# Reordering the first five blocks of a fused dynamic convolution and squared-ReLU FFN: one load, one exp and the softmax and product steps between the units

## The chip, the cores and the metric

One core of one Trainium2 chip runs the whole program. The metric is the device time of one execution in microseconds (us). A run has a median over three to eleven executions. Ratios compare the runs of two kernels in the same rounds, so they are not quite the ratio of the medians that are quoted beside them. Each has a 95% interval. "The changed kernel" is the kernel after the change, "before" the kernel before it.

## The reference

```python
w = exp(weight_gen - max); w = w / (sum(w) + 1e-9)           # (8, 4096, 8 heads, 7 taps)
out[b,s,h,g] = sum_k w[b,s,h,k] * x_pad[b, s+k, h, g]        # causal window of 7, D = 192
h = maximum(out.reshape(32768, 192) @ w_in, 0.0)             # (192, 2048)
y = (h * h) @ w_out                                          # (2048, 192), float32 out
```

## The kernel before

The 32,768 tokens are cut into 64 sub-blocks of 512. Blocks 0 and 1 hold one sub-block, every later one two. One block goes through these steps:

- softmax of a part of `weight_gen` on ScalarE (exp, "E") and VectorE (sum, reciprocal, scale, "S"). The result `v` is moved as rows into `wr` by DMA;
- VectorE multiplies `wr` with a mask into bands `bd` ("B" and the sub-block's number);
- TensorE multiplies bands with x into `yp` ("C"), ScalarE copies it to `y`;
- 16 units "u" (8 in blocks 0 and 1): TensorE makes `h`, ScalarE the ReLU `t`, VectorE the square `g`;
- "M": TensorE multiplies half of the hidden tiles `g` of 256 tokens with `w_out` into `o`, as a rule for an earlier block; after every second M ScalarE copies one PSUM bank out and VectorE adds the other (blocks 0 and 1 use one bank and need no sum).

The digit after E, S, L (load) is the softmax part. Plans fix the order by hand for the first blocks, and all engines work through their share of that order without skipping ahead. A ring is a pool of buffers used in turn: who wants the next buffer waits until its last reader is done. The gate is a one-column copy on GpSimd that waits for a load and so holds back the loads that GpSimd issues after it. What the argument touches:

```python
p_t1 = ctx.enter_context(tc.tile_pool(name="p_t1", bufs=5))      # the t ring
ps_h = ...(name="ps_h", bufs=3, space=PSUM)                      # h and yp share three slots
ps_o = ...(name="ps_o", bufs=1, space=PSUM)                      # one pair of o banks
# ... start of the program, after the weights of part 0 and w_in ...
        x_load_f32(1)                                   # second x, sync queue
        nc.scalar.copy(out=w_i[:, 1, 0], in_=w_st[1])
        cross_w_in(1)
        s1.load(nc.sync)                                # weights of softmax part 1
        for i in (0, 2, 1, 3, 4):
            st_band(0, (i,))
        st_conv(0)                                      # C of block 0, then the first y copy
        nc.gpsimd.tensor_copy(out=gate, in_=x_st[1][:, 0:1])   # GpSimd waits for the second x
        for q in range(4):
            load_w_out(q, 4)                            # 1.5 MB, GpSimd queue, behind the gate
        s2.load(nc.gpsimd)
        x_load(2)
# ... a softmax part that is done: its rows go to wr on the sync and the GpSimd queue in turn
        move_rows(s)
# a unit
        nc.scalar.activation(out=t1, in_=h, func=ActF.Relu)
        nc.vector.tensor_tensor(out=g, in0=t1, in1=t1, op=AluOp.mult)
```

The softmax here doesn't subtract the row's maximum and nothing guards it: scores larger than these inputs give would overflow.

Of the kernel before, what the change touches and what calls it, by code (L numbers as in the profile page):

```python
# [9 lines left out]
def kernel(  # L10
# [26 lines left out]
    nc = tc.nc  # L37
# [96 lines left out]
    def cross_w_in(q):  # L134
        for r0, r1 in ((0, RT), (RT, 0)):
            nc.sync.dma_start(out=w_i[r0 : r0 + RT, q, 1], in_=w_i[r1 : r1 + RT, q, 0])

    def cross_w_in_by_pe(q):
        n = NQ + NQ // 2
        for a in range(0, n, 2 * TB):  # L140
            b = min(a + 2 * TB, n)
            pt = ps_h.tile([P, 2 * TB], f32, name="pt", tag="h")
            for c in range(a, b, TB):
                nc.tensor.matmul(
                    out=pt[:, c - a : c - a + TB], lhsT=swap, rhs=w_i[:, q, 0, c : c + TB],
                    start=True, stop=True,
                )
            nc.scalar.copy(out=w_i[:, q, 1, a:b], in_=pt[:, 0 : b - a])
# [137 lines left out]
    def block_load(j, dst, src, width, eng):  # L286
        t0 = (j % NBB) * TB
        first, last = int(t0 == 0), NT
        if first:
            eng.dma_start(out=dst[:, 0], in_=src[0:P, :])  # L290
        a = t0 + tile_start(j, NT - 1)
        if a != t0 + starts[-1]:
            last = NT - 1
            eng.dma_start(out=dst[:, last], in_=src[a : a + P, :])
        ap = rows(src, t0 + starts[first], width)
        ap = bass.AP(
            tensor=ap.tensor, offset=ap.offset,
            ap=[ap.ap[0], [STEP * width, last - first], ap.ap[2]],
        )
        eng.dma_start(out=dst[:, first:last], in_=ap)  # L300
# [5 lines left out]
    def x_load_f32(j):  # L306
        x_st[j] = p_one.tile([P, (R + HALO) * HK], f32, name="x_st", tag="ex")
        block_load(
            j, x_st[j][:, 0 : NT * D].rearrange("p (t d) -> p t d", t=NT), x[j // NBB], D, nc.sync
        )  # L310
# [199 lines left out]
    with nc.allow_low_precision("fp16 matmul pipeline"), tc.manual_schedule():  # L510
# [26 lines left out]
        def spin(n):  # L537
            for i in range(n):
                nc.tensor.matmul(out=wp, lhsT=warm[:, 0:P], rhs=warm, start=True, stop=True)  # L539

        s0, s1, s2 = parts[:3]
# [19 lines left out]
        x_cast(0, nc.scalar.copy)  # L561
        cross_w_in_by_pe(0)
        spin(14)
        x_load_f32(1)
        nc.scalar.copy(out=w_i[:, 1, 0], in_=w_st[1])
        cross_w_in(1)
        s1.load(nc.sync)
        for i in (0, 2, 1, 3, 4):
            st_band(0, (i,))
        st_conv(0)  # L570
# [2 lines left out]
        for q in range(4):  # L573
# [6 lines left out]

        steady = "MuMuuu" * 3 + "MuuuMCu"
        plans = {
            0: "B1 X1 u u u E1 S1 u C u u u u",
            1: "L3 u u B2 M E2 B3 u M E2 u u S2 u M u C u S2 M",
            2: "L4 u u u E3 M u u u M B4 u u u u M B5 S3 u u u u M u E3 C u",
            3: "L5 L6 M S3 u u u M u u u u M u M B6 E4 u u u M M B7 u u S4 u E4 M u C M u",
        }


# [45 lines left out]
        for j in range(len(plans), NBLK):  # L635
            plan, u = [], 0
# [55 lines left out]
        for j in range(NBLK):  # L692
            if j + 2 < NBLK:
                load_rows(j + 2)
            u = 0
# [71 lines left out]
```

## Time and profile before

| | before |
|---|---|
| time, median of 3 (lowest to highest) | 748.35 us (748.23 to 749.56) |
| span of the profiled execution | 746.6 us |
| first unit of block 0 begins at | 15.55 us |
| blocks 0, 1, 2, 3, 4, 5 take | 8.03, 13.25, 18.12, 22.63, 23.40, 22.52 us |
| a steady block | 22.55 us |

A block's time is the distance from its first matmul of the plan to the next block's. TensorE is the bound, so what a block takes over the pace of its matmuls shows as a TensorE wait, whose releaser names who caused it, or as a slot that is longer than usual (the view of waits leaves out gaps under 0.15 us).

### The profile page before, as it was taken

What the parts mean: (1) busy time and instruction counts of PE and PEld (TensorE: products, weight loads), DVE (VectorE), ACT (ScalarE), POOL (GpSimd) and SP (SyncE); (2) the same over time, 40 slices, a digit from 0 to 9 for tenths busy, and PEclk for the clock granted to TensorE, in tenths of its full rate; (3) what the DMA queues carried; (4) which work ended last, traced back from release to release, by engine and by line L of the source; (5) the groups of instructions that cost most, each with busy time, mean ns of one, the idle gap of its engine ahead of it and who ended that gap; (6) DMA issues with size and microseconds to landing.
All of it is one profiled execution on the core that took longest, in us unless ns stands there. A gap on an engine that the chain in (4) does not pass through costs nothing.

```text
span 746.6 us, 33289 instructions
## 1 busy us (share of the span) xinstructions
PE 739.0 (99%) x15106; PEld 556.5 (75%) x15106; DVE 621.8 (83%) x1001; ACT 624.7 (84%) x755; POOL 88.8 (12%) x130
## 2 busy tenths in 40 slices
PE   8999999999999999999999999999999999999998
PEld 4767877877777777777777777787777777777787
DVE  5999998998889888888889888898888987677853
ACT  5998788888888888888888888888888888888874
POOL 7321220101101100011000110001100011001000
PEclk9999999999999999999999999999999999999999
DMA  8654454436554234644245542365441354441312
GB/s 223 112 106 109 80 101 85 100 70 139 94 118 79 75 57 80 140 79 73 45 74 139 102 65 53 51 139 108 59 80 48 57 108 80 60 73 51 51 46 65
DMA packets 122169, 64.81 MB, mean 87 GB/s; under 512 B 83849, under 2 KB 118636, under 8 KB 121516
## 3 DMA queue, kind: packets, MB, share of 16 engines
q1 hardware_dynamic: 77708, 45.66, 22.4%
q0 software_dynamic: 44176, 16.93, 20.5%
q8 instruction: 118, 1.93, 1.1%
q14 instruction: 23, 0.19, 0.1%
q10 hardware_dynamic: 144, 0.10, 0.0%
HBM read 48.61 MB, written 28.70 MB: 104 GB/s over the span
## 4 chain that ended last, share of the span: by engine, by line
PE 94%; DVE 2%; issue 1%; DMA 1%; ACT 1%; POOL 0%; DVEq 0%; ACTq 0%
PE o L475 45%; PE h L441 43%; PE yp L416 6%; DVE g L453 1%; DVE bd L348 1%; DMA wr<-v_first 0%; DMA wg<-in_weight_gen_dram 0%; POOL wr L330 0%; ACT t L450 0%; DVE v_first L239 0%; ACT ex L217 0%; DVE ssum L224 0%; DVE rcp L231 0%; DVE o_sb L491 0%; ACT y L427 0%
## 5 line engine op out<-in xcount | busy, mean ns | idle before, releaser
L450 ACT ACTIVATE t<-h 128x1024 f16<-128x1024 f32 x512 | 496.7, 1026 | 65.6 <-PE h L441 65.3
L453 DVE TENSOR_TENSOR g<-t 128x1024 f16<-128x1024 f16 x512 | 334.3, 687 | 100.5 <-ACT t L450 97.8
L475 PEld LDWEIGHTS <-g 64*128 64x128 f16 (+1 forms) x8032 | 352.3, 94 | 55.0 <-issue 4.8
L475 PE MATMUL o<-w_o,g 64*128 64x192 f16 (+1 forms) x8032 | 385.3, 243 | 0.9 <-DVE o_sb L491 0.6
L441 PE MATMUL h<-y,w_i 64*128 64x512 f16 (+1 forms) x3168 | 379.7, 370 | 2.2 <-ACT t L450 0.9
L441 PEld LDWEIGHTS <-w_i 64*128 64x128 f16 x3168 | 162.6, 94 | 117.2 <-issue 5.2
L348 DVE TENSOR_TENSOR bd<-wr,mask 128x4160 f16<-128x4160 f16 (+3 forms) x89 | 149.3, 1701 | 4.0 <-DMA wr<-v_first 4.0
L300 POOL DMA_DIRECT2D xt<-in_x_dram x62 | 51.2, 830 | 446.7 <-PE yp L416 423.7
L489 ACT COPY o_sb<-o 128x384 f32<-128x384 f32 x129 | 62.2, 482 | 33.8 <-PE o L475 33.8
L491 DVE TENSOR_TENSOR o_sb<-o,o_sb 128x384 f32<-128x384 f32 x123 | 68.2, 555 | 8.4 <-ACT o_sb L489 5.6
L427 ACT CAST y<-yp 128x1024 f16<-128x1024 f32 (+1 forms) x64 | 48.1, 803 | 14.5 <-PE yp L416 14.5
L416 PE MATMUL yp<-bd,xt 128*32 128x104 f16 (+8 forms) x3864 | 51.7, 208 | 0.3 <-DVE bd L348 0.2
L416 PEld LDWEIGHTS <-xt 128*32 128x32 f16 (+3 forms) x3864 | 46.2, 92 | 6.7 <-issue 6.2
L239 DVE TENSOR_TENSOR v_big<-ex,rcp 128x112 f16<-128x112 f32 (+1 forms) x136 | 27.3, 263 | 1.8 <-DMA vd<-v_big 0.6
L217 ACT ACTIVATE ex<-wg 128x448 f32<-128x448 f32 (+2 forms) x44 | 27.2, 618 | 1.8 <-DMA wg<-in_weight_gen_dram 1.8
L224 DVE TENSOR_REDUCE ssum<-ex 128x64 f32<-128x448 f32 (+2 forms) x44 | 26.1, 594 | 2.5 <-ACT ex L217 2.3
L231 DVE RECIPROCAL rcp<-ssum 128x64 f32<-128x64 f32 (+2 forms) x44 | 23.7, 539 | 1.5
L290 POOL DMA_DIRECT2D xt<-in_x_dram x7 | 3.8, 549 | 135.8 <-PE yp L416 135.8
L330 POOL DMA_DIRECT2D wr<-v_first x31 | 16.8, 561 | 16.3 <-DVE v_first L239 16.1
L539 PE MATMUL wp<-warm 128*128 128x512 f16 x39 | 11.4, 459 | 1.3 <-DVE warm L531 1.3
L539 PEld LDWEIGHTS <-warm 128*128 128x128 f16 x39 | 4.3, 114 | 7.6 <-issue 3.5
L239 DVE TENSOR_TENSOR v_first<-ex,rcp 128x112 f16<-128x112 f32 (+1 forms) x48 | 9.1, 255 | 0.3
(24 smaller groups left out, 28.2 us busy)
## 6 DMA issues: line engine op xcount, KB each, us to landing
out_dram<-o_sb SPq DMA_DIRECT2D x63, 384.0 KB, 3.0
xt<-in_x_dram POOLq DMA_DIRECT2D x42, 240.0 KB, 5.9
wg<-in_weight_gen_dram SPq DMA_DIRECT2D x4, 1064.0 KB, 8.3
xt<-in_x_dram POOLq DMA_DIRECT2D x20, 192.0 KB, 5.6
wr<-vd SPq DMA_DIRECT2D x38, 80.0 KB, 3.6
vd<-v_big SPq DMA_DIRECT2D x5, 512.0 KB, 5.5
wg<-in_weight_gen_dram SPq DMA_DIRECT2D x5, 392.0 KB
wg<-in_weight_gen_dram SPq DMA_DIRECT2D x3, 616.0 KB, 4.1
```

What stands on the lines that cost most here:

```text
L217: nc.scalar.activation(out=self.ex[:, lo:hi].rearrange("p r g k e -> p (r g) k e"), in_=self.wg[:, lo:hi].rearrange("p r (g e) k -> p (r g ...
L239: eng.tensor_tensor(out=bass.AP(tensor=v.tensor, offset=v.offset + lo * H * SL + lo % SL * 2 + g * SL * 2, ap=[list(v.ap[0]), [H * SL + 2, ...
L300: eng.dma_start(out=dst[:, first:last], in_=ap)
L348: nc.vector.tensor_tensor(out=bd_t[j][:, H * lo : H * (lo + len(tiles) * n)].rearrange("p (g m c) -> p g m c", g=shape[1], c=2 * SL), in0= ...
L416: nc.tensor.matmul(out=yps[k // per][p0 : p0 + m, col + a : col + b], lhsT=x_t[s][:, i, 32 * q : 32 * q + m], rhs=bd[:, h // 2, h % 2, a - ...
L427: nc.scalar.copy(out=y[:, k0:k1, 0:th], in_=yp[:, 0 : (k1 - k0) * th].rearrange("p (k c) -> p k c", c=th),)
L441: nc.tensor.matmul(out=h[:, half, jj * th : (jj + 1) * th], lhsT=w_in_chunk(u * per + jj, slot, half), rhs=y_t[j][r0 : r0 + RT, k, 0:th], ...
L450: nc.scalar.activation(out=t1, in_=h, func=ActF.Relu)
L453: nc.vector.tensor_tensor(out=g, in0=t1, in1=t1, op=AluOp.mult)
L475: nc.tensor.matmul(out=oo[:, cc * Dm : (cc + 1) * Dm], lhsT=g[r0 : r0 + n, cc * P : (cc + 1) * P], rhs=w_o[r0 : r0 + n, fc, :], start=(fc ...
L489: nc.scalar.copy(out=o_sb, in_=o[0][:, c])
L491: nc.vector.tensor_tensor(out=o_sb, in0=o[1][:, c], in1=o_sb, op=AluOp.add)
```

## The change

The intent: load the weights of part 1 earlier, so that their exp leaves ScalarE's busy stretch in block 0, and spread the steps of blocks 1 to 4 better. The whole diff:

```diff
         spin(14)
+        s1.load(nc.sync)
         x_load_f32(1)
         nc.scalar.copy(out=w_i[:, 1, 0], in_=w_st[1])
         cross_w_in(1)
-        s1.load(nc.sync)
+        s1.exp(0, s1.rh)
         for i in (0, 2, 1, 3, 4):
             st_band(0, (i,))
@@ plans
-            0: "B1 X1 u u u E1 S1 u C u u u u",
-            1: "L3 u u B2 M E2 B3 u M E2 u u S2 u M u C u S2 M",
-            2: "L4 u u u E3 M u u u M B4 u u u u M B5 S3 u u u u M u E3 C u",
-            3: "L5 L6 M S3 u u u M u u u u M u M B6 E4 u u u M M B7 u u S4 u E4 M u C M u",
+            0: "B1 X1 S1 u u u u C u u u u",
+            1: "L3 u M E2 B2 u B3 u M S2 u u u M u E2 C u S2 M",
+            2: "L4 u u u E3 S3 u E3 M u M u B4 B5 S3 u u u M u u u u M u C u M u",
+            3: "L5 L6 u u u M E4 B6 u u u M M S4 u u u M E4 M B7 u u u M u S4 C u M u u",
+            4: "u M u M B8 u u u M u u M u B9 E6 u u u M M u C M S6 E5 u u E5 u M S5 u",
```

Before, plan 4 was made by the rule for steady blocks ("MuMuuu" three times, then "MuuuMCu", with the softmax steps put in between).

## The prediction

> **What bounds the kernel now.** I read the engine shares first, then who waited for whom, then busy time by stage, then the instructions in order of time in the first 80 us. A "unit" below is one hidden-layer tile: matmuls into h, the ScalarE pass h to t, the VectorE square t to g. "M" is half a quarter of the second product (o), "C" a block's convolution matmuls (yp), "B" a band build (bd), "E" and "S" the exp and the rest of one softmax piece.
>
> The page's first part, with busy time, share and count by engine:
> ```profile
> PE 739.0 (99%) x15106; PEld 556.5 (75%) x15106; DVE 621.8 (83%) x1001; ACT 624.7 (84%) x755; POOL 88.8 (12%) x130
> ```
> TensorE is the bound over the whole run: there is matmul work nearly everywhere, and only a TensorE wait can be won back. The view of waits lists all of those after the warm-up:
> ```profile
> PE h L441 <- ACT t L450: 0.9, 1, 0.9
> PE h L441 <- ACT y L427: 0.9, 1, 0.9
> PE o L475 <- DVE o_sb L491: 0.6, 1, 0.6
> ```
> These, and some short slots that are filled at ScalarE's pace, are all the change can win. A whole steady block takes 22.55 us from its first matmul to the next block's (169.09 to 191.62, for example). Busy time by stage; the stretches are blocks 0, 1, 2, 3 and 4, and the columns are length, then each engine's busy us:
> ```profile
> 15.55:23.58 8.03, 6.88 (x168) 6.00 (x168) 7.61 (x17) 7.17 (x9) 3.99 (x6) 1.00 1.32 220
> 23.58:36.83 13.25, 13.16 (x282) 10.85 (x281) 13.03 (x21) 12.12 (x15) 5.91 (x10) 1.00 0.44 73
> 36.83:54.95 18.12, 18.12 (x283) 10.79 (x284) 16.74 (x30) 17.02 (x21) 3.39 (x7) 1.00 0.50 100
> 54.95:77.58 22.63, 22.63 (x475) 16.56 (x472) 21.12 (x37) 20.18 (x26) 6.32 (x11) 1.00 0.46 99
> 77.58:100.98 23.40, 22.78 (x475) 19.41 (x473) 21.66 (x40) 19.66 (x25) 3.35 (x7) 1.00 0.36 63
> ```
> VectorE (the third figure after the length) is busy 7.61 of 8.03, 13.03 of 13.25 and 16.74 of 18.12 us: through blocks 0 to 2 it is full, behind a TensorE that only just does not wait for it. Block 4 holds the 0.6 us wait for o_sb and is 0.85 us over steady.
>
> From the timeline, the ScalarE and VectorE rows that the sums below use (start, duration, what):
> ```profile
> 14.70 0.80 ACT L427 CAST y<-yp 128x768 f16<-128x768 f32 x1 [1.92 <-PE yp L416]
> 17.17 0.65 DVE L314 CAST xt<-x_st 128x960 f16<-128x960 f32 x1
> 19.14 0.95 ACT L217 ACTIVATE ex<-wg 128x784 f32<-128x784 f32 x1
> 20.12 0.97 DVE L224 TENSOR_REDUCE ssum<-ex 128x112 f32<-128x784 f32 x1
> 23.39 3.69 DVE L453 TENSOR_TENSOR g<-t 128x1024 f16<-128x1024 f16 x6
> 27.84 4.59 DVE L348 TENSOR_TENSOR bd<-wr,mask 128x4160 f16<-128x4160 f16 x3
> 34.15 0.61 DVE L224 TENSOR_REDUCE ssum<-ex 128x64 f32<-128x448 f32 x1
> 37.94 0.50 DVE L224 TENSOR_REDUCE ssum<-ex 128x48 f32<-128x336 f32 x1
> 44.72 2.32 DVE L348 TENSOR_TENSOR bd<-wr,mask 128x4160 f16<-128x4160 f16 x1
> 52.77 1.58 PE L416 MATMUL yp<-bd,xt 128*32 128x104 f16 x120
> 78.43 1.48 PE L475 MATMUL o<-w_o,g 64*128 64x192 f16 x31 [0.62 <-DVE o_sb L491]
> ```
>
> **What the Trainium skill says.** "Perfetto Trace Analysis", section Identifying the Most-Contended Engine, warns that matmul busy time flatters TensorE. The trace agrees (weight loads 75% against 99%), so I count waits and slot lengths, not the share. The same page, Optimization Strategy, says that a kernel can have regimes with different most-contended engines: here the first 55 us are VectorE's. The same page, Optimizing Scalar/DVE Operations, says that an instruction's profiled latency exceeds the time it holds the engine. It agrees: six g take 3.69 us and a lone one 0.69, so one holds VectorE 0.60. "DMA: Bandwidth & Descriptors", section Anatomy of one DMA, gives about 2.0 us plus bytes over 436 GB/s, an estimate of 2.9 us for the 392 KB weight load; the first one here took 3.1 us from issue to its exp, later ones 4.4 to 6.6 us.
>
> **The change part by part.** No arithmetic is added or removed; ScalarE, VectorE and TensorE run the same instructions in another order.
>
> 1. Load and exp of part 1. Its load goes from 14.0 us to 10.3 us on the sync queue, ahead of the second x. Estimated landing is 10.3 + 3.1 to 4.4 = 13.4 to 14.7. The exp (0.95) was in ScalarE's stream at 19.14, in a stretch where TensorE runs at ScalarE's pace; it now stands in a 1.92 us ScalarE gap before the first y copy at 14.70. Gain 0.95 us if the load lands by 13.7; none if it lands at 14.7, since y is then late by as much. The second x goes 0.6 us later, and its cast at 17.17 should still find it.
>
> 2. S1 goes ahead of the first g. From 17.74, when x is cast, VectorE does S1 (20.12 to 23.39 = 3.27 us) and then g. The first g ends near 21.7. The t ring has 5 buffers, so the sixth t waits 0.2 us. The first M comes one unit earlier, which fills a slot that ran at ScalarE's pace (0.27 us over). I put block 2's start at 35.8, 1.0 us ahead of 36.83.
>
> 3. Block 2. Both S3 pieces now lie in it ahead of C, the second straight behind B4 and B5; before, the second piece lay in block 3. VectorE's queue from 17.74 to the g of the seventh unit of block 2, in its time per item: S1 3.27; 22 g by 0.60 = 13.2; B2 and B3 27.84 to 32.35 = 4.51, B4 and B5 as much; S2 in two pieces 1.99 + 1.65 (34.15 to 36.14, 37.94 to 39.59), S3 as much. Sum 32.77, so 50.5 without any wait. The queue before, up to B4, adds up to 17.74 + 24.6 = 42.4 where the trace shows 44.72, so 2.3 us of waits for ScalarE. With E1 and S1 early I take 1.0 us. The seventh g then ends at 51.5 + 0.69 = 52.2. The twelfth t uses its buffer's place again, so it runs 52.3 to 53.3. C takes the PSUM slot of the twelfth h (three slots), so it starts at 53.4 at the latest reckoning, 53.1 with 0.3 us less waiting.
>
>    TensorE would like C earlier: from 35.8, 14 units by 0.65 = 9.1, four M with both switches by 1.52 = 6.1, 0.1 before C: 51.1. So C waits about 2.0 us. The next unit needs the slot of the one before C, whose t ends after two more t and an o copy: another 0.6 us. Block 2 loses 2.6 us against 1.0 won, and block 3 starts 1.6 us late for the same work.
>
> 4. Block 3 and 4. VectorE catches up in block 3, since the second S3 piece has gone from it. The wait for o_sb in block 4 comes from an M that opens a quarter one unit after the one that closed the last. Its slot took 2.11 us where 1.32 is usual. In the new plans this pair has three units between it, so 0.79 us is won. But block 4 now ends "M S5 u" and block 5 opens with an M that needs the same bank: o copy 0.48, sum 0.55 and hand-overs 0.3 against a unit of 0.65, about 0.7 us lost at the start of block 5.
>
> Sum: -1.0 + 2.6 - 0.8 + 0.7 = +1.5 us, on 748.35: 749.8 us. Blocks 5 to 32 are unchanged.
>
> **Rivals.** (a) The change does what it says: no VectorE queue in front of C, E1 off the path, the o_sb wait gone. That gives -1.0 - 0.8 to -1.8 us, near 746.8. For it: VectorE had 1.4 us idle in block 2 before, and someone placed these steps by hand. Against it: 6.2 us of B4, B5 and S3 in a row with five t and three h buffers to bridge them, about 8 units by 0.65. (b) The load lands late, or 392 KB more in flight at 10 to 15 us delays the rows for the first bands (B1 waited 0.73 us for them before). VectorE's chain then begins later by up to 0.8 us and C with it: 750.6. The early exp alone hardly matters then, because C is timed by VectorE and not by ScalarE. (c) B8 comes sooner after S4 and could find its rows not landed; the moves took 81.12 to 85.4, and I count 6.8 us from S4 to B8 where about 6.3 are needed. A miss costs VectorE a few tenths, and the t ring hides that.
>
> **Range and chances.** The rivals span 746.8 to 750.6, and the three runs before spread over 1.3 us, so I take 747.3 to 751.3 for eight times in ten. 2% is 15 us; all TensorE waits in the first five blocks do not reach 5 us, and the new ones need more than three times my sum to reach it. Faster by 2% 0.005, within 0.985, slower 0.01.
>
> **What would show it.** Step 1: the exp at or before 14.7, the y copy no later than 14.8, and no exp between the third and fourth t. Step 2: block 2's first unit near 35.8. Step 3: a TensorE wait of about 2 us at yp near 51 to 53, its releaser ScalarE's t, behind a VectorE with no gap from 17 to 52; block 3's first unit near 57.9 after one M more than before. Step 4: no o_sb wait near 78 and one near 101 to 102; block 5 starting near 101.7. I am wrong if VectorE shows gaps before 50 us, if C does not wait, or if the bands at 14.9 slip by over 1 us.

## The result, and the profile after

| | before | after |
|---|---|---|
| median of 4 | 748.29 us (747.95 to 749.56) | 752.74 us (752.00 to 753.22) |
| ratio | | 1.0055 [1.0038, 1.0073] |
| span of the profiled execution | 746.6 | 750.5 |

The changed kernel is slower by 0.55%, about 4.1 us. Within 2% this is "same", but it is clear of the noise. The engine shares nearly hide it, as this line of the page of the changed kernel shows against its counterpart in the prediction:
```profile
PE 738.9 (98%) x15106; PEld 557.1 (74%) x15106; DVE 621.8 (83%) x1001; ACT 624.8 (83%) x755; POOL 89.5 (12%) x130
```
The work is the same to 0.1 us on three engines. The 4 us are waits. Here is the changed kernel's view of waits (engine, line, what it waited for: us in total, times, longest). From the first unit on TensorE's waits are all here, with three waits of the engines that feed it:
```profile
POOL wr L330 <- DMA w_o<-in_moe_w_out_dram: 1.3, 1, 1.3
DVE bd L348 <- DMA wr<-v_first: 7.1, 3, 4.1
ACT t L450 <- DVE g L453: 3.4, 3, 2.9
PE yp L416 <- ACT t L450: 1.8, 1, 1.8
PE yp L416 <- DVE bd L348: 1.7, 2, 1.4
PE h L441 <- ACT y L427: 0.9, 1, 0.9
PE h L441 <- ACT t L450: 0.6, 1, 0.6
PE o L475 <- DVE o_sb L491: 0.6, 1, 0.6
PE o L475 <- ACT o_sb L489: 0.5, 1, 0.5
```
Against before, TensorE has three new waits at yp and h (1.8, 1.4 and 0.6 us), and the wait for o_sb now comes twice. To place them, this is the view by stage of the changed kernel for blocks 0 to 5, with the same columns as in the prediction:
```profile
16.34:23.63 7.29, 6.90 (x169) 6.01 (x169) 7.22 (x17) 6.42 (x8) 6.93 (x10) 1.00 0.95 112
23.63:38.58 14.95, 13.46 (x281) 11.01 (x281) 12.33 (x20) 12.10 (x15) 4.44 (x8) 1.00 0.63 105
38.58:60.61 22.03, 19.57 (x314) 12.39 (x314) 20.35 (x40) 17.82 (x22) 7.92 (x14) 1.00 0.48 82
60.61:81.85 21.24, 21.24 (x443) 15.90 (x440) 19.54 (x35) 18.85 (x24) 0.68 (x2) 1.00 0.42 105
81.85:105.00 23.15, 22.70 (x474) 16.57 (x471) 18.90 (x31) 20.66 (x27) 6.24 (x10) 1.00 0.57 87
105.00:128.43 23.43, 22.84 (x472) 19.29 (x473) 22.96 (x45) 19.09 (x24) 3.03 (x6) 1.00 0.25 76
```
Block 2 now holds one M more and block 3 one M less, 1.32 us each. With that put back, the ledger of the two profiles is:

| block | before | after | difference |
|---|---|---|---|
| 0 | 8.03 | 7.29 | -0.74 |
| 1 | 13.25 | 14.95 | +1.70 |
| 2, less one M | 18.12 | 20.71 | +2.59 |
| 3, plus one M | 22.63 | 22.56 | -0.07 |
| 4 and 5 | 45.92 | 46.58 | +0.66 |
| sum | 107.95 | 112.09 | +4.14 |

The sum agrees with the ratio (0.0055 of 748.3 is 4.1). The first unit also begins 0.8 us later (16.34 against 15.55), but that is not shown to be part of the change. Two runs further down (e3, e11) have the same first 16 us of program as before and began at 16.17 and 16.00; the profile of before was an early one. From block 6 to the end this profile of before happened to take 1.0 us more than that of the changed kernel, so the two spans differ by 3.9 us.

The chain of waits of the changed kernel between 25 and 60 us (start, duration, what the end hung on) shows how the losses of blocks 1 and 2 hang together:
```profile
18.89 6.44 DMA w_o<-in_moe_w_out_dram
25.34 0.28 issue
25.62 4.88 DMA wr<-v_first
...
32.75 2.27 DVE bd L348 x2
...
47.77 4.59 DVE bd L348 x3
...
54.71 0.56 ACT t L450
...
58.00 0.82 PE h L441 x6
```
In order of time: a w_out load, the rows for a band behind it, VectorE's bands, softmax pieces and squares without a break up to 54 us, one t, and then TensorE. In the kernel before, the same view has TensorE on the chain from 24.5 to 70 us. The row transfer on the chain is the last of part 1 (for B3, landed at 30.50); what left VectorE idle was B2, whose own rows let it start at 29.82.

How the w_out load came to be late, and what B2 waited, is in these lines of the two timelines (start, duration, what, and the wait in brackets). Before:
```profile
14.66 0.18 POOL L572 COPY gate<-x_st 128x1 f32<-128x1 f32 x1 [2.30 <-DMA x_st<-in_x_dram]
```
After:
```profile
16.16 1.23 POOL L573 COPY gate<-x_st 128x1 f32<-128x1 f32 x1 [3.75 <-DMA x_st<-in_x_dram]
17.34 3.04 POOL L161 DMA_DIRECT2D w_o<-in_moe_w_out_dram  x4
29.82 2.33 DVE L348 TENSOR_TENSOR bd<-wr,mask 128x4160 f16<-128x4160 f16 x1 [2.55 <-DMA wr<-v_first]
```
Of the 2.55 us by which w_out is issued later (14.79 before), 1.5 come from the second x, which landed that much later. The other 1.05 are the gate's copy: it took 1.23 in place of 0.18 us. It began while VectorE was building B1 (15.46 to 17.35) and ended 0.04 us after that. In all eleven profiles of this case in which the gate's copy began during a VectorE band it ended 0.04 to 0.05 us after the band; in the other seven it took 0.18. While w_out was held back, the DMA engines moved nothing from 17.0 to 18.7 us (0 GB/s in the view of DMAs of 14 to 31 us; the kernel before and e4 have no such hole).

### The profile page after: what moved, and what is told of

Read it like the earlier page. It is cut to its first block, busy times and chain, and to the rows that moved or that the text cites. A ratio compares the mean times of both kernels' runs of the same rounds, so it can differ in the third digit from the quotient of the medians.

```text
span 750.5 us, 33287 instructions
## 1 busy us (share of the span) xinstructions
PE 738.9 (98%) x15106; PEld 557.1 (74%) x15106; DVE 621.8 (83%) x1001; ACT 624.8 (83%) x755; POOL 89.5 (12%) x130
## 4 chain that ended last, share of the span: by engine, by line
PE 90%; DVE 4%; DMA 3%; issue 1%; ACT 1%; SPq 1%; POOL 0%; DVEq 0%; ACTq 0%
PE o L475 43%; PE h L441 41%; PE yp L416 6%; DVE g L453 1%; DVE bd L348 1%; DMA w_st<-in_moe_w_in_dram 1%; DMA w_o<-in_moe_w_out_dram 1%; DMA wr<-v_first 1%; ACT t L450 1%; DMA w_i<-w_i 0%; DVE v_first L239 0%; DVE rcp L231 0%; DVE ssum L224 0%; SPq L129 0%; ACT w_i L566 0%
## 5 line engine op out<-in xcount | busy, mean ns | idle before, releaser
L416 PE MATMUL yp<-bd,xt 128*32 128x104 f16 (+7 forms) x3864 | 52.3, 208 | 3.9 <-ACT t L450 1.8
```

The source lines that it names most:

```text
L416: nc.tensor.matmul(out=yps[k // per][p0 : p0 + m, col + a : col + b], lhsT=x_t[s][:, i, 32 * q : 32 * q + m], rhs=bd[:, h // 2, h % 2, a - ...
```

## The experiments

Each was built from one of the two kernels with the edit shown, was correct, and was timed in five rounds. Runs e1 to e4, e5 to e8, e9 to e12 and e13 to e16 are each on one chip with its own runs of before; runs are compared by their ratios to before, whose intervals are about 0.003 wide. The figures per block come from the one profile of each run. In the profiles of e5, e15 and e16 the granted clock was 0.82, 0.79 and 0.81 over block 0, where before and after show 1.00, and two units there took 1.23 to 1.28 us in place of 0.65. Their block 0 took 8.21 to 8.22 us (in e16 B1 also waited 2.56 us for its rows) and is not used below.

**e1: the early load alone** (from before).
```diff
+        s1.load(nc.sync)
         x_load_f32(1)
 ...
-        s1.load(nc.sync)
```

> The kernel before with one edit: the weight load of part 1 is issued ahead of the second x; exp, S1 and all plans as before. Row theory (the load delays the second x, that delays the gate and the w_out loads behind it, and those delay the rows for the bands of blocks 1 and 2): slower than before by 1.0 to 2.5 us, first unit about 0.5 us later, w_out issued near 17 instead of 14.8, VectorE waiting for wr rows near 27 to 29. Rival (the order of VectorE's steps in the new plan 1 makes the wait): within 0.3 us of before apart from what the first unit loses.

Measured: 748.84 us against 748.72; ratio 0.9999 [0.9986, 1.0012]. A miss for the row theory in its time, though its parts on gate and rows came true: the gate opened at 16.44 in place of 14.66, w_out was issued at 17.47 in place of 14.79, and VectorE waited 0.76 us for rows before B2. But C in the old plan 1 came only after that, and did not wait more than 0.3 us. So the late rows are harmless here, where nothing else has become earlier.

**e2: the new start and plan 0, plans 1 to 4 of before** (from before).
```diff
+        s1.load(nc.sync)
         x_load_f32(1)
 ...
-        s1.load(nc.sync)
+        s1.exp(0, s1.rh)
 ...
-            0: "B1 X1 u u u E1 S1 u C u u u u",
+            0: "B1 X1 S1 u u u u C u u u u",
```

> The start and plan 0 of the changed kernel (early load, early exp, S1 ahead of g), plans 1 to 4 of before. Row theory: the wait of C for its bands near 33 stays, block 1 is 1.5 us or more over before's 13.24, in all slower than before by 1.0 to 2.0 us. Rival (order in plan 1): block 1 as before, in all 0.5 to 1.0 us faster than before. Neither theory has a C wait on a t in block 2.

Measured: 749.37 us; ratio 1.0006 [0.9992, 1.0019]. Neither expectation was right in size. Block 0 took 7.23 us, so the start wins the 0.8 us it was meant to win. Block 1 took 14.12, so all of it is lost there: VectorE waited 1.6 us for rows before B2, and C took 2.38 us in place of 1.5. So the start alone makes a wait at C in block 1, without the new plan 1, but only half of the loss: 0.87 us, where the changed kernel lost 1.70. The rest needs the new plan 1 as well, in which VectorE comes to B2 earlier and waits 2.55 us.

**e3: the new plans 1 to 4, start and plan 0 of before** (from after: the edit of e2 taken back).

> The start and plan 0 of before, plans 1 to 4 of the changed kernel. VectorE queue theory (the second S3 piece behind B4 and B5 ahead of C): C of block 2 waits about 1.8 us and the next unit 0.6 for a t, block 2 is 2.3 to 2.9 us over before for the same work; rows land in time, so C of block 1 waits under 0.3 us. With the o_sb wait moved and not removed: slower than before by 2.3 to 3.3 us. Rival (C of block 2 waits only because block 1 was late): within 0.7 us of before.

Measured: 751.23 us; ratio 1.0033 [1.0020, 1.0046], so 2.5 us slower, as the VectorE theory had it. Rows came in time (C of block 1 took 1.52). Block 2, less one M, took 20.34, which is 2.2 over before. The rival falls: block 2 loses this without any lateness from block 1.

**e4: the gate on another tile** (from after).
```diff
-        nc.gpsimd.tensor_copy(out=gate, in_=x_st[1][:, 0:1])
+        nc.gpsimd.tensor_copy(out=gate, in_=s1.wg[:, 0, 0, 0:1])
```

> The changed kernel with one edit: the gate that holds back the w_out loads reads the weights of part 1 (landed by 14.2) and not the second x (landed at 16.2). Row theory: w_out issued near 14.5 to 15, rows of blocks 2 and 3 land before 28, C of block 1 waits under 0.5 us; faster than the changed kernel by 1.2 to 2.2 us, so slower than before by 2.0 to 3.0. Rival (VectorE's order in plan 1): no change, slower than before by about 4.

Measured: 751.40 us; ratio 1.0033 [1.0020, 1.0045]. w_out was issued at 14.56, VectorE's wait for rows before B2 fell from 2.55 to 0.34 us, C of block 1 took 1.51 and block 1 12.98 in place of 14.95. One line that touches only the time of the w_out loads (and of the two loads behind them on GpSimd's queue) takes away the whole loss of block 1. VectorE's order was untouched, so the rival falls.

The rows themselves, by the view of DMA issues between 14 and 31 us (source, queue, count, KB each, median us from issue to landing). Before:
```profile
wr<-v_first SPq DMA_DIRECT2D x5, 16.0 KB, 2.1
wr<-v_first POOLq DMA_DIRECT2D x4, 16.0 KB, 1.7
```
After:
```profile
wr<-v_first SPq DMA_DIRECT2D x5, 16.0 KB, 5.8
wr<-v_first POOLq DMA_DIRECT2D x4, 16.0 KB, 5.5
```
Transfers of 16 KB take three times as long on both queues alike. Their data is the same. What is new: S1 is done earlier, so the rows start at 21.88 and not at 23.49, and the last of the w_out loads, issued 2.5 us later, lands at 26.41 and not at 22.77, with the weights and x behind it. In e4 the last w_out load landed at 23.87 and the rows still took 4.1 and 3.9 us, but that was early enough for B2. (The last row transfer on GpSimd's queue was also issued 1.25 us late. In the trace its instruction waits for the semaphore of the third w_out load, so this wait belongs to the built program; B3, which needs that row, did not wait.)

**e5: the second S3 piece back in block 3** (from after).
```diff
-            2: "... B4 B5 S3 u u u M ..."          3: "L5 L6 u u u M ..."
+            2: "... B4 B5 u u u M ..."             3: "L5 L6 S3 u u u M ..."
```

> The changed kernel with the second S3 piece moved from behind B5 in block 2 to the start of block 3, where it was before. VectorE queue theory: the C of block 2 and the unit after it no longer wait for a t; block 2 takes 2.2 to 2.6 us less than the changed kernel's 22.03; the kernel is faster than the changed one by 1.8 to 2.6 us, so slower than before by 1.5 to 2.3. Rival (C of block 2 waits because block 1 ended late, or because of E3 on ScalarE): block 2 stays over 21.5 us, the time stays about 4 us over before.

Measured: 754.38 us; ratio 1.0079 [1.0062, 1.0096], no better than the changed kernel (that it is worse is not shown: the intervals overlap). A miss. Block 2 did get shorter, from 22.03 to 20.37. Block 3 grew from 21.24 to 23.65. From the timeline of this run, an M of block 3 that waits for VectorE's sum (start, duration, what, and the wait in brackets); another waited 0.49 us at 64.28:
```profile
70.58 2.80 PE L475 MATMUL o<-w_o,g 64*128 64x192 f16 x63 [1.54 <-DVE o_sb L491]
```
S3 now stands ahead of squares and of the sum that frees the o banks, and its rows are late for B6, which waited 1.70 us. The wait moved with the work. It is not enough to take a step from a full queue; the place where it goes must have room.

**e6: eight t buffers** (from after).
```diff
-    p_t1 = ...(name="p_t1", bufs=5)
+    p_t1 = ...(name="p_t1", bufs=8)
```

> The changed kernel with 8 buffers for t in place of 5, order of work untouched. If the wait passes from VectorE to TensorE through the t ring (ScalarE may not write a sixth t before the first is squared), ScalarE no longer waits for a g near 52 to 55 and the C of block 2 starts without its 1.8 us wait: faster than the changed kernel by 1.8 to 2.6 us. Rival (C waits for the bands B4 and B5 themselves, or VectorE's queue delays what TensorE needs in another way): block 2 stays within 0.5 us of the changed kernel's.

Measured: 749.92 us; ratio 1.0033 [1.0015, 1.0052], 1.6 us less than the changed kernel's by the two ratios (they are from different calls), a little under the 1.8 to 2.6 expected. Block 2 fell from 22.03 to 19.89. The waits of this run that answer to those of the changed kernel:
```profile
PE yp L416 <- DVE bd L348: 1.4, 2, 1.1
ACT t L450 <- DVE g L453: 0.2, 1, 0.2
```
Of ScalarE's waits for a square (3.4 us) 0.2 is left, and that of C for a t (1.8 us) is gone; C's wait for its bands in block 1 stays. The order of VectorE's work is the same as in the changed kernel, so the t ring is what carried VectorE's lag to TensorE.

**e7: the last M of block 4 two units earlier** (from after).
```diff
-            4: "... C M S6 E5 u u E5 u M S5 u"
+            4: "... C M S6 E5 u M E5 u u S5 u"
```

> The changed kernel with the last M of block 4 two units earlier, so that three units and not one stand between it and the M that opens block 5. If that pair waits for the o bank: no wait for o_sb near 105, blocks 4 and 5 together 1.1 to 1.4 us shorter, faster than the changed kernel by 1.0 to 1.4 us, so slower than before by 2.7 to 3.2. Rival (M waits because VectorE is late there, with S6 and S5 around it): the wait stays over 0.5 us.

Measured: 752.58 us; ratio 1.0068 [1.0053, 1.0084], not better than the changed kernel. A miss. Block 4 fell to 22.54, and the M that opens block 5 no longer waited, but the second M of block 5 took 2.55 us in place of 1.32: 1.1 us of it was a wait for a square, because S5 stands ahead of the last squares of block 4. The rival, VectorE late there, was right.

**e8: the mends of e4, e5 and e7 together** (from after; the three edits above).

> The changed kernel with all three mends: gate on the weights of part 1, second S3 piece in block 3, last M of block 4 two units earlier. If the three losses are separate and add up, with the 0.75 us of block 0 kept: 1.6 + 2.3 + 1.2 off the changed kernel's 4.1 over before, so faster than before by 0.5 to 1.7 us. If they hide each other (one wait behind another), less is won, and the kernel ends above before.

Measured: 752.79 us; ratio 1.0069 [1.0052, 1.0087]. A miss, and it follows from e5 and e7: block 1 was mended (12.98), while blocks 3 (23.46) and 5 (24.35) lost as in those runs.

**e9: plan 4 in the steady order** (from after).
```diff
-            4: "u M u M B8 u u u M u u M u B9 E6 u u u M M u C M S6 E5 u u E5 u M S5 u"
+            4: "M E6 u M S6 u u u M u M B8 u u u M E5 u M B9 u u u M E5 u u u M C S5 u"
```

> The changed kernel with plan 4 written in the order that the steady blocks have (M u M u u u and so on, C near the end), all else as changed. If the loss at the turn from block 4 to 5 comes from what plan 4 packs at its end (S6, the exps, S5 and one unit between two M), the last unit of block 4 and the first M of block 5 take 0.66 and 1.32 us in place of 1.26 and 2.08, blocks 4 and 5 together 45.1 to 45.4 in place of 46.6: faster than the changed kernel by 1.0 to 1.6 us. Rival (the loss is carried in from blocks 1 to 3, which were late): it stays, 46 us or more.

Measured: 750.85 us; ratio 1.0035 [1.0016, 1.0053]. Blocks 4 and 5 together took 45.09 in place of 46.58. The loss was made inside plan 4 and not carried in: blocks 4 and 5 took 46.6 us also in e3, e4, e6 and e15, which keep plan 4 and enter it 1.8 to 3.1 us earlier than the changed kernel (e3 at 80.10 and e6 at 79.14, against 81.85). The profile of the changed kernel shows how:
```profile
103.15 0.52 ACT L217 ACTIVATE ex<-wg 128x336 f32<-128x336 f32 x1
103.55 1.03 ACT L450 ACTIVATE t<-h 128x1024 f16<-128x1024 f32 x1
104.46 0.49 ACT L489 COPY o_sb<-o 128x384 f32<-128x384 f32 x1
105.00 0.24 PE L475 MATMUL o<-w_o,g 64*128 64x192 f16 x1 [0.45 <-ACT o_sb L489]
105.22 0.55 DVE L491 TENSOR_TENSOR o_sb<-o,o_sb 128x384 f32<-128x384 f32 x1
```
The o copy of the closing M stood behind the exp of part 5 and a t on ScalarE. The first matmul of the next M waited 0.45 us for the copy, the rest another 0.6 for VectorE's sum after it. In this run's profile block 0 took 8.03 us and C of block 1 did not wait, so it does not tell what the start costs on the average.

**e10: new start, gate as in e4, plans 1 to 4 of before** (from e2 with the edit of e4).

> The new start and plan 0 with the gate on the weights of part 1, and plans 1 to 4 of before. If the start's gain is real and only the late rows ate it: block 0 at 7.2 to 7.3, block 1 at 13.0 to 13.3 with no wait of C, faster than before by 0.4 to 1.0 us. Rival (the early load itself makes the start later by as much): within 0.2 us of before.

Measured: 747.84 us; ratio 0.9991 [0.9977, 1.0006]: 0.7 us faster, but not clear of the noise. Its profile fell on an execution in which the rows of the first bands landed late: B1 waited 1.95 us for them, the squares came late and block 0 took 8.53. The new start has this weakness: S1 stands ahead of the squares on VectorE, so what delays B1 and the x cast delays the squares of block 0.

**e11: before with eight t buffers.** The edit of e6, from before.

> The kernel before with 8 buffers for t, as a control for the next run. Before shows no ScalarE wait for a g over 0.3 us, so the ring does not bind it: within 0.3 us of before. Rival (a longer ring helps everywhere, and the gain of 8 buffers in the changed kernel is not about its block 2): faster by over 1 us.

Measured: 748.31 us; ratio 0.9998 [0.9983, 1.0014]. The ring alone is worth nothing where VectorE does not lag.

**e12: gate, eight t buffers and steady plan 4 together** (from after; the edits of e4, e6 and e9).

> The changed kernel with gate on the weights of part 1, 8 buffers for t, and the steady plan 4. Sum of the blocks as the single runs gave them, against before: block 0 -0.75, block 1 -0.25, block 2 +0.3, block 4 -0.85: faster than before by 0.8 to 1.9 us. Rival (as with the three earlier mends together, a loss mended shows up in the next block): within 0.5 us of before or slower.

Measured: 747.51 us; ratio 0.9987 [0.9971, 1.0003]. By blocks 0, 1, 2, 3 and 4 with 5 against before: 7.23, 12.99, 18.60, 22.57 and 45.19, in sum 106.58 and 1.37 less. Its interval still touches 1. In the view of waits of this run TensorE has none left for a t or for o_sb; the 0.9 us for the first y is there.

Four more runs on one chip:

**e13: the changed kernel again**, unedited.

> The changed kernel once more, unedited, so that the next three stand beside it on one chip and its first trace has a second. Slower than before by 3.5 to 4.8 us. If the wait of C in block 1 belongs to the change and not to one execution, C of block 1 again takes over 2.2 us and the first w_out load is issued after 16.5; block 2 again 21.5 to 22.1.

Measured: 753.09 us; ratio 1.0061 [1.0049, 1.0074]. C of block 1 took 3.01, w_out was issued at 17.72, block 2 took 22.02: the losses belong to the change and not to one execution.

**e14: e4 again.**

> The gate on the weights of part 1 beside the changed kernel on one chip: faster than the changed kernel by 0.8 to 1.8 us, C of block 1 at 1.5 to 1.6, w_out issued near 14.5, rows landed in under 5 us. If the first comparison was chance, it is within 0.5 us of the changed kernel.

Measured: 751.44 us; ratio 1.0021 [1.0006, 1.0036]. Beside e13 it is faster by 1.7 us in the median and 2.6 in the mean; the blocks of the two profiles differ by 2.1 us in sum. In its profile VectorE waited 0.97 us for rows before B2 and C took 1.90 and block 1 13.38, so the gate does not free the rows fully in every execution.

**e15: e4 and e6 together.**

> Gate on the weights of part 1 and 8 buffers for t, plan 4 as changed. If the losses of blocks 1 and 2 are separate, their mends add: 1.2 to 1.7 and 1.6 to 2.1 off the changed kernel, which leaves 0 to 1.2 us over before, all of it from blocks 4 and 5. If one hides the other: 2 us or more over before.

Measured: 749.45 us; ratio 1.0000 [0.9987, 1.0014]. The two mends add up and bring the kernel back to before.

**e16: e12 again.**

> The kernel with all three mends (gate, 8 buffers, steady plan 4) once more, since its interval touched 1: faster than before by 0.6 to 1.6 us with an interval below 1 if the sum of blocks holds; within 0.4 us if the first was chance.

Measured: 747.50 us; ratio 0.9979 [0.9966, 0.9991]. The version with all three mends beats the kernel before by 1.0 to 1.6 us (the two runs) and the changed kernel by about 6 us (e13 beside e16).

## Why the prediction was right or wrong

The sign was right and so was the longest term, but two terms were wrong and the time fell outside the range. The prediction summed to +1.5 us where +4.1 was measured.

- **Step 1, load and exp.** The exp ran at 14.20, inside the span foreseen, and no exp stands between the t of block 0 any more. Block 0 gained 0.74 where 0.95 was foreseen. But "The second x goes 0.6 us later, and its cast at 17.17 should still find it" was followed only as far as the cast. The x was issued 0.7 us later, landed 1.5 us later, and the gate waits for the same tile. It opened at 16.16 and its copy held GpSimd for 1.23 us, so w_out was issued at 17.34 in place of 14.79, and the rows of S1 ran into it. **This is the first step that failed.** e4 shows it, as it moves nothing but the gate and the loads behind it. The condition on the exp ("none if it lands at 14.7, since y is then late by as much") did not bite here, where y waited for C until 15.45. In five other profiles with the early exp (e5, e7, e8, e15, e16) C was done by 14.8, the exp held y for 0.5 to 0.7 us, and TensorE's wait for the first y was 1.3 to 1.6 us in place of 0.9.
- **Step 2, block 2's start.** 35.8 was foreseen and 38.58 came. In blocks 0 and 1 the prediction had 1.0 us won; the ledger has 0.96 lost. The difference of 2.0 us is C's wait for bands in block 1 (C took 3.39 in place of 1.51). The rival (b) named the contention, but at the first bands and with 0.8 us. In the profile of the changed kernel it was the right mechanism at the wrong place: the band that was hit was B2, where VectorE stood idle for 2.55 us, while B1 waited 0.49. In other executions the first bands are hit too: B1 waited 0.34 to 0.73 us in the three profiles with the old order of loads, and longer than that in 11 of the 15 with the early load, up to 2.56 (e16). The prediction's own sign of being wrong, "if VectorE shows gaps before 50 us", came true with B2.
- **Step 3, block 2.** Right in mechanism and size: 2.6 foreseen, 2.59 measured, with a wait at C whose releaser is ScalarE's t (1.8 us) and one at the next unit (0.6). e3 gives 2.2 for the same step without the late rows, and e6 shows that the t ring carries it. C came at 55.78 and not near 53, since VectorE lost 2.55 us at B2; TensorE entered block 2 late by the same cause, so the difference stood. In e4, where B2 waits 0.34 us, C came at 53.16, where 53.1 to 53.4 was foreseen, and block 2 lost 2.4. So the size was not luck. (VectorE was called full "through blocks 0 to 2" and the first 55 us VectorE's. In block 2 before, it was busy 16.74 of 18.12 us and TensorE for all 18.12; the new order filled that slack and went over it.)
- **Step 4, blocks 4 and 5.** The wait at the start of block 4 did go, and a new one came at the end, as foreseen. Its size was wrong. **This is the second step that failed:** 0.7 us was reckoned for copy, sum and hand-overs, as if ScalarE were free. The M that opens block 5 and the unit ahead of it took 2.08 and 1.26 us in place of 1.32 and 0.65, so 1.37. The copy stood behind an exp and a t; e9, which gives plan 4 the steady order, has 1.32 and 0.66 there. Blocks 3 to 5 together gave +0.6 in place of -0.1.
- **Rival (a)**, all won and nothing lost, was wrong for this kernel, but e12 and e16 come near its number with three mends added. **Rival (c)**, rows late for B8, did not show: VectorE's three row waits in that profile lie at the first bands, at B1 and at B2 (4.07, 0.49 and 2.55 us).
- **The sum.** 1.5 and the two failed terms, 2.0 and 0.7, make 4.2. Two slips in it cost nothing: 169.09 to 191.62 is 22.53 and not 22.55, and rival (a), 1.8 under 748.35, is 746.55 and not 746.8.

What stays open: the first unit began at 15.55 to 16.17 us in three profiles with the same first 16 us of program, and with the new start a late B1 takes back part of block 0's gain (7.74 to 8.53 us in e7, e9, e10 and e13). What it costs on the average is not shown, as each run has one profile.

## What to carry to other kernels

When a load is moved ahead of another, follow the one that is passed to everything that waits for it, including gates and the loads behind them; here the loss came three hand-overs later, at a band of the next block. Look also at what runs beside a small step on that path: the gate's copy lasted as long as the VectorE band that it fell into. An engine that is off the bound but full has a queue, and the rings between it and the bound say how much lag they bridge: five t buffers did not bridge B4, B5 and S3 in a row, eight did. Moving a step out of such a queue only helps if the place it goes to has slack, and the release of a shared bank counts every item ahead of the copy in that engine's order, not the copy alone.

## What the Trainium skill lacked or had wrong

- "DMA: Bandwidth & Descriptors", section Anatomy of one DMA: 2.0 us plus bytes over 436 GB/s, given for the GpSimd path, makes an estimate of 2.04 us for 16 KB. The row transfers on GpSimd's queue come near it before (median 1.7 us). Those of the changed kernel took 5.5 beside other loads, and the fit has no term for that. The section Issuing engines are not separate DMA queues, by which DMAs of all issuers interleave on the same engines, fits better: both queues slowed alike (5.8 on the sync queue).
- "Perfetto Trace Analysis", section Optimization Strategy, ties a lack of buffers to a bubble that repeats. Here a single bubble of 1.8 us had that cause, and three more buffers removed it (e6).
